# A fused attention and MLP layer on one core: a new lead-in, projections over pairs of blocks, and a new order of instructions

## The chip, the cores and the metric

The kernel runs on one NeuronCore of a Trainium2 chip. The metric is the device time of one execution in microseconds, the median of several. A profile shows the span from the first to the last instruction of one execution; the device time is some 2.6 us longer (215.04 against a span of 212.4 here).

Names of the engines: PE is TensorE (matrix products; PEld its weight loads), DVE is VectorE, ACT is ScalarE, POOL is GpSimd, SP is SyncE, which here only issues DMAs.

## The reference: what is computed

```python
S, D, F, H, W, dil = 2048, 640, 1536, 32, 8, 2      # bf16 inputs
xn  = layernorm(x)                                  # (x - mean) / sqrt(var + 1e-5), no scale or shift
qkv = xn @ wqkv                                     # [2048, 1920], 32 heads of 20
# each position attends to itself and to 7 earlier ones, 2 apart (masked where before the start)
logits[h, s, w] = q[h, s] . k[h, s - 2*w] * 20**-0.5
o[h, s] = sum_w softmax_w(logits)[h, s, w] * v[h, s - 2*w]
out = x + o @ wo + gelu_tanh(xn @ w1 + b1) @ w2 + b2
```

The two branches, attention and MLP, share the normalised input and are added to the residual x.

## The kernel before

The 2048 rows are cut into four chunks of 512 rows, and each chunk into four blocks of 128. Work on TensorE is in bf16 with the contraction over five slices of 128 columns (KT = 5). After normalisation, a block has to be transposed so that the 640 columns lie on the partitions: in chunk 0 by TensorE (`tp`) and a copy out of PSUM (`tc`), in chunks 1 to 3 by a transposing DMA (`td`).

The loads at the start, in the order of issue:

```python
    nc.sync.dma_start(x_sb[:, 0, :], x_nb[:, 0, :])          # block 0
    nc.scalar.dma_start(x_sb[:, 1, :], x_nb[:, 1, :])        # block 1, another queue
    for s in range(3):                                       # q, k, v: 800 KB each
        nc.sync.dma_start(wqkv[s][:], wqkv_v[:, :, s * D : (s + 1) * D])
        if s == 1:
            nc.sync.dma_start(x_sb[:, 2:BPC, :], x_nb[:, 2:BPC, :])
    nc.sync.dma_start(b1_rt[0:FT, :], ...)
    for cs in (slice(BPC, 2 * BPC), slice(2 * BPC, NCH * BPC)):   # blocks 4-7, 8-15
        nc.sync.dma_start(x_sb[:, cs, :], x_nb[:, cs, :])
    nc.sync.dma_start_transpose(b1_t[:], b1_rt[:])
    nc.sync.dma_start(w1_sb[:], ...)                         # all of w1, 1920 KB
    # ... w2, wo and b2 are loaded later, after chunk 1's transposes
```

The normalisation and the transposes of chunk 0, a block at a time (`bn_stats`/`bn_aggr` on VectorE, root on ScalarE, reciprocal and normalisation on VectorE):

```python
    def do_tp(n, bl, a, b):
        xn = tiles["xn", n, bl]
        tp = get(("tp", n, bl), lambda: psA.tile([P, 2 * CH], BF16, tag="acc", name="tp"))   # one tile a block
        for t in range(a, b):
            nc.tensor.transpose(tp[:, t * P : (t + 1) * P], xn[:, t * P : (t + 1) * P], ident[:])

    def do_tc(n, bl, a, b):
        ...
        nc.scalar.copy(xnT[:, a:b, bl * P : (bl + 1) * P], tiles["tp", n, bl][:, a * P : b * P]...)
```

The projections of chunk 0 go a block at a time, each matmul with 128 moving columns; five groups of output tiles per block:

```python
GROUPS = (((0, 0, 4),), ((1, 0, 4),), ((0, 4, 5), (1, 4, 5)), ((2, 0, 4),), ((2, 4, 5),))   # (q/k/v, from, to)

    def do_gj(bl, g, a, b):
        cs = slice(bl * P, (bl + 1) * P)
        ps = get(("gps", bl, g), lambda: psA.tile([P, BPC, P], F32, tag="acc", name="gps"))
        ...
            nc.tensor.matmul(ps[:, i, :], lhsT=wqkv_p[which][:, ti, to, :],
                             rhs=tiles["xnT", 0][:, ti, cs], start=..., stop=...)
```

In chunks 1 to 3 a projection (`pj`) and in all chunks the first MLP layer (`f1`) are groups of five matmuls with 512 moving columns. The output of a block (`o`) is 17 matmuls of 512 (`lo`) and 17 of 128 (`hi`): 12 for the MLP's second layer and 5 for wo. VectorE multiplies q by shifted k (`qk`), TensorE sums the heads (`lg`, tile `L`), VectorE and ScalarE make the softmax, the attention is expanded over the partitions by a DMA (`xd`, `xs`), VectorE multiplies it with shifted v (`av`) and adds (`ad`, `ot`).

Before everything 44 matmuls on zeros (`idle`) keep TensorE busy until the first data arrive; the zeros are written by VectorE:

```python
    zeros = consts.tile([P, P], BF16, name="zeros")
    nc.vector.memset(zeros[:], 0.0)
    ...
        for _ in range(WARM):                                # 44
            nc.tensor.matmul(idle[:, 0, :], lhsT=zeros[:], rhs=zeros[:], start=True, stop=True)
```

The residual goes to the output by DMA: x is stored (`xp`), the bias b2 is added to it in DRAM by an accumulating DMA (`xb`), and each block's result is added in the same way (`od`). The last block instead adds on VectorE and is stored.

The order of all these pieces on every engine is not written by hand. A planner in the kernel (`Plan`) holds each piece with an estimated duration, a rank, what it needs and which buffers it holds; it walks through time, starts on each engine the piece of lowest rank that can start, and the kernel's instructions are emitted in that order. Each engine then runs its instructions in exactly this order and waits where something isn't ready.

```python
RANK = {"av1": 36.4, "av2": 74, "f12": 4.1, ..., "xn0": -14.7}     # 21 offsets, by kind of piece and chunk
    for name, n in (
        ("acc", 4), ("L", 1), ("O", 1), ("xnT", 3), ("q", 2), ("k", 2), ("v", 2), ("prod", 4),
        ("e", 1), ("attn", 1), ("ax", 1), ("oT", 1), ("hT", 18), ("osb", 2), ("xn", 2), ...
```

`acc` are the four PSUM banks that projections, first layer and transposes share; `L` and `O` are for logits and outputs.

Of the kernel before, what the change touches and what calls it, by code (L numbers as in the profile page):

```python
# [15 lines left out]
PE, VE, SE, DQ = "pe", "ve", "se", "dq"  # L16


class Plan:
# [8 lines left out]
    LAG = {PE: 0.22, VE: 0.08, SE: 0.1, DQ: 0.0}  # L28
# [4 lines left out]

    def pool(self, name, n):
        self.pools[name] = n

    def add(self, name, engine, us, rank, needs, fn, bufs=(), after=0.0, table=None, slack=0.0):
        t = {
            "name": name,
            "eng": engine,  # L40
            "us": us,
            "rank": rank + self.offsets.get(name[: 4 if name[:2] in ("pj", "pc", "ad") else 3], 0.0),
            "needs": list(needs),
            "fn": fn,
            "bufs": list(bufs),
            "after": after,
            "table": table,
            "slack": slack,
            "i": len(self.tasks),
        }  # L50
        self.tasks.append(t)
        self.by[name] = t
        for b in bufs:
            self.bufs.setdefault(b, set()).add(name)
        return name

    def run(self):
        end, left, held = {}, list(self.tasks), {p: {} for p in self.pools}
        remaining = {b: set(u) for b, u in self.bufs.items()}
        free = {PE: 0.0, VE: 0.0, SE: 0.0, DQ: 0.0}  # L60
        now, started, table = 0.0, [], "sqrt"
        running, slacks = [], {t["slack"] for t in self.tasks}
        while left:
            done = [t for t in running if t["end"] <= now + 1e-9]
# [7 lines left out]
            while moved:  # L72
                moved = False
                for eng in (PE, VE, SE, DQ):
# [34 lines left out]
            nxt = [f for f in free.values() if f > now + 1e-9]  # L109
            for late in slacks:  # L110
# [20 lines left out]
EPS = 1e-5  # L131
MASKED = -1e9
# [4 lines left out]
GROUPS = (((0, 0, 4),), ((1, 0, 4),), ((0, 4, 5), (1, 4, 5)), ((2, 0, 4),), ((2, 4, 5),))  # L137
# [4 lines left out]
    "av1": 36.4, "av2": 74, "f12": 4.1, "f13": 69.4, "gj1": 19.4, "gj2": -19.4, "o02": -8.9, "o10": 15.3,  # L142
    "o12": -3.3, "o13": -11.3, "o20": 117, "o31": 57.5, "o33": 85.2, "ot0": 20, "pj22": -106.4, "pj31": -13.1,
    "qk1": -4.8, "qk2": 4.4, "st2": 164.2, "st3": 219.3, "xn0": -14.7,
# [3 lines left out]
def make_plan(fns, offsets=RANK):  # L148
# [10 lines left out]

    def done(n, which):  # L160
        if n:
            return [f"pc{n}{which}{to}" for to in range(KT)]
        return [f"gc{bl}{g}" for bl in range(BPC) for g, parts in enumerate(GROUPS) if which in [p[0] for p in parts]]

    pl.add("b1", VE, 0.1, -90, [], f("b1"), after=21.0)
    for n in range(NCH):
# [6 lines left out]
        for bl in range(BPC):  # L173
            land = (4.0, 4.0, 9.6, 9.6)[bl] if n == 0 else (0.0, 13.3, 17.1, 17.1)[n]
            r = -40 if n else -99
            pl.add(f"st{n}{bl}a", VE, 0.5, r, [], f("st", n, bl, 0), after=land)
            pl.add(f"st{n}{bl}", VE, 0.62, r, [f"st{n}{bl}a"] + ([f"rc{n}{bl - 1}"] if n == 0 and bl else []), f("st", n, bl, 1))
            if n == 0:
                pl.add(f"rs{n}{bl}", SE, 0.35, -99, [f"st{n}{bl}"], f("sqrt", n, bl, bl + 1), table="sqrt")
                pl.add(f"rc{n}{bl}", VE, 0.17, -99, [f"rs{n}{bl}"], f("rstd", n, bl, bl + 1))  # L180
# [3 lines left out]
        for bl in range(BPC):  # L184
            xn, tp = ("xn", n, bl), ("acc", "tp", n, bl)
            if n > 0:
                pl.add(f"xn{n}{bl}", SE, 0.81, early + -4.0, [f"rc{n}"], f("xn", n, bl), [xn])
                pl.add(f"tc{n}{bl}", DQ, 4.0 if n > 1 else 2.7, early - 3.0, [f"xn{n}{bl}"], f("td", n, bl), [xn, xnT], 21.5)
                continue

            for i, (a, b) in enumerate(((0, 2), (2, KT)) if bl == 0 else ((0, KT),)):
                u = "a" if b < KT else ""
                us = (b - a) / KT
                pl.add(f"xn{n}{bl}{u}", VE, 0.06 + 0.36 * us, -99, [f"rc{n}{bl}"], f("xn", n, bl, a, b), [xn])
                pl.add(f"tp{n}{bl}{u}", PE, (0.54 if bl == 0 else 0.3) * us, -99, [f"xn{n}{bl}{u}"], f("tp", n, bl, a, b), [xn, tp])
                pl.add(f"tc{n}{bl}{u}", SE, 0.16 + 0.49 * us, -99, [f"tp{n}{bl}{u}"], f("tc", n, bl, a, b), [tp, xnT])
        if n == 1:
            pl.add("ld", DQ, 9.2, -1000, [f"tc1{bl}" for bl in range(BPC)], f("ld"))
        pl.add(f"xp{n}", DQ, 0.3, base + 30, ["ld"], f("xp", n))
        pl.add(f"xb{n}", DQ, 0.0, base + 33, [f"xp{n}"], f("xb", n))  # L200

        if n == 0:
            for bl in range(BPC):
                for g, parts in enumerate(GROUPS):
                    ps, last = ("acc", "g", bl, g), max(p[0] for p in parts)
                    tos = sum(p[2] - p[1] for p in parts)
                    land = (6.4, 8.7, 11.8)[last]
                    r = -50 + (last == 2)
                    need, cut = [f"tc0{bl}"], 0
                    if bl == 0 and g == 0:  # L210
                        cut = 2
                        need.append(pl.add("ga00", PE, 0.112 * tos, r, ["tc00a"], f("gj", bl, g, 0, cut), [xnT, ps], land))
                    pl.add(f"gj{bl}{g}", PE, 0.056 * (KT - cut) * tos, r, need, f("gj", bl, g, cut, KT), [xnT, ps], land)
                    pl.add(f"gc{bl}{g}", SE, (0.27, 0.54, 0, 0.54)[tos - 1], -50, [f"gj{bl}{g}"], f("gc", bl, g), [ps] + [(q, k, v)[p[0]] for p in parts])
# [543 lines left out]
```

## Time and profile before

| | |
|---|---|
| device time, median of 3 runs | 215.04 us (214.53 to 215.87) |
| span of the profiled execution | 212.4 us |
| TensorE busy | 206.9 us (97%) |
| VectorE busy | 174.4 us (82%) |
| ScalarE busy | 109.5 us (52%) |
| DMA traffic | 23.95 MB, mean 113 GB/s |
| granted TensorE clock | 1.000 |

The profile is a page with: the busy time of each engine; the span in 40 slices, each digit the busy share of a slice in tenths; the chain of work that ended last, followed back from the last instruction to what released it; and groups of instructions by line of the kernel, with what ended the idle time before them. The trace behind it can be asked for a timeline: start and length in us, engine, line, operation, output<-inputs, number of instructions, and in square brackets the idle time before them and what ended it. A line such as L501 is a line of the kernel; L501 is the matmul of `do_gj`, L484 of `do_pj`, L653 of `do_f1`, L684 and L686 of `do_o`, L557 of the logits, L437 the transposes, L725 the matmuls on zeros.

### The profile page before, as it was taken

To read this page: it belongs to the slowest core of one execution; us is meant where nothing else is said; L and a number is where in the kernel's file an instruction comes from. 1 tells how busy PE (TensorE), PEld (TensorE's weight loads), DVE (VectorE), ACT (ScalarE), POOL (GpSimd) and SP (SyncE) were. 2 spreads that over 40 slices of the span, in tenths; PEclk is the share of its full clock that TensorE was granted. 3 is DMA by queue.
4 is the path that set the end of the run, shared out by engine and by line. 5 is a ranking of instruction groups with operands and counts; after the bars stand their busy time and mean duration, and the time that the engine had idled before them with its cause. 6 is when DMAs were issued, how large, how long until landed. Compare 5 with 4: busy or idle time off the path is not lost.

```text
span 212.4 us, 3961 instructions
## 1 busy us (share of the span) xinstructions
PE 206.9 (97%) x1670; PEld 121.7 (57%) x1693; DVE 174.4 (82%) x178; ACT 109.5 (52%) x193; POOL 19.7 (9%) x37
## 2 busy tenths in 40 slices
PE   8999999999999999999999999999999999999994
PEld 8799845655545555555555555455555455555552
DVE  3579999759999997599996999999999999972001
ACT  3568997798574654931353883503752511341120
POOL 2000000000020024101100010101110011101130
PEclk9999999999999999999999999999999999999999
DMA  6999528916829199993120027202114611122214
GB/s 216 365 362 376 93 50 275 322 24 132 206 64 163 37 287 196 197 195 89 15 30 0 0 31 200 31 3 31 14 21 48 180 19 22 27 29 31 34 16 76
DMA packets 23465, 23.95 MB, mean 113 GB/s; under 512 B 9112, under 2 KB 20632, under 8 KB 23448
## 3 DMA queue, kind: packets, MB, share of 16 engines
q1 hardware_dynamic: 17864, 16.49, 28.3%
q0 software_dynamic: 4144, 4.92, 17.2%
q10 hardware_dynamic: 1440, 2.29, 3.9%
q8 instruction: 13, 0.21, 0.4%
q14 instruction: 4, 0.03, 0.1%
HBM read 10.00 MB, written 7.54 MB: 83 GB/s over the span
## 4 chain that ended last, share of the span: by engine, by line
PE 97%; issue 1%; DVE 0%; ACT 0%
PE lo L684 27%; PE hps L653 24%; PE pps L484 23%; PE gps L501 8%; PE hi L686 8%; PE L L557 4%; PE idle L725 2%; PE tp L437 1%; ACT xnT L441 0%; DVE osb L714 0%; DVE zeros L361 0%
## 5 line engine op out<-in xcount | busy, mean ns | idle before, releaser
L653 PE MATMUL hps<-xnT,w_sb 128*128 128x512 bf16 x235 | 54.1, 379 | 0.3
L684 PE MATMUL lo<-w_sb,hT 128*128 128x512 bf16 x183 | 51.8, 379 | 0.0
L631 DVE TENSOR_TENSOR pv<-vT,ax 128x2560 bf16<-128x2560 bf16 x32 | 45.9, 1484 | 1.7 <-PE L L557 1.7
L535 DVE TENSOR_TENSOR prod<-qT,kT 128x2560 bf16<-128x2560 bf16 x32 | 45.4, 1484 | 0.0
L686 PE MATMUL hi<-w_sb,hT 128*128 128x128 bf16 x192 | 40.3, 219 | 0.6 <-issue 0.2
L664 ACT ACTIVATE hT<-hps,b1T 128x512 bf16<-128x512 f32 x48 | 31.6, 687 | 17.0 <-PE hps L653 13.3
L653 PEld LDWEIGHTS <-w_sb 128*128 128x128 bf16 x240 | 23.0, 98 | 26.7
L640 DVE TENSOR_TENSOR pv<-pv 128x5120 bf16<-128x5120 bf16 x12 | 33.9, 2825 | 0.4
L684 PEld LDWEIGHTS <-hT 128*128 128x128 bf16 x192 | 18.7, 98 | 22.8 <-issue 0.6
L691 ACT CAST osb<-lo 128x512 bf16<-128x512 f32 x15 | 8.8, 585 | 44.0 <-issue 28.0
L697 POOL DMA_DIRECT2D out_dram<-osb x15 | 12.9, 863 | 110.5 <-ACT osb L692 110.5
L684 PE MATMUL lo<-wo,oT 128*128 128x512 bf16 x79 | 23.0, 379 | 0.0
L686 PEld LDWEIGHTS <-hT 128*128 128x128 bf16 x192 | 18.4, 98 | 1.5
L398 DVE BATCH_NORM_STATS2 stats<-x_sb 128x6 f32<-128x320 bf16 x32 | 14.0, 469 | 5.1 <-DMA x_sb<-in_A_x_dram 5.1
L484 PE MATMUL pps<-xnT,wq_sb 128*128 128x512 bf16 x71 | 16.9, 380 | 0.2
L484 PE MATMUL pps<-xnT,wv_sb 128*128 128x512 bf16 x73 | 16.9, 379 | 0.1
L686 PE MATMUL hi<-wo,oT 128*128 128x128 bf16 x80 | 16.9, 219 | 0.1
L484 PE MATMUL pps<-xnT,wk_sb 128*128 128x512 bf16 x73 | 16.8, 379 | 0.1
L705 DVE TENSOR_TENSOR osb<-lo,x_sb 128x512 bf16<-128x512 f32 x1 | 0.7, 692 | 16.1 <-PE lo L684 16.1
L520 ACT CAST qT<-pps 128x512 bf16<-128x512 f32 x15 | 8.8, 585 | 9.2 <-PE pps L484 9.2
L684 PEld LDWEIGHTS <-oT 128*128 128x128 bf16 x80 | 7.8, 98 | 9.4
L484 PEld LDWEIGHTS <-wk_sb 128*128 128x128 bf16 x75 | 8.7, 118 | 7.3 <-issue 0.2
(62 smaller groups left out, 205.9 us busy)
## 6 DMA issues: line engine op xcount, KB each, us to landing
w_sb<-in_B_w_dram SPq DMA_DIRECT2D x2, 1920.0 KB, 9.2
out_dram<-osb POOLq DMA_DIRECT2D x15, 160.0 KB, 3.4
ax<-attn SPq DMA_DIRECT2D x8, 256.0 KB, 5.4
ax<-attn ACTq DMA_DIRECT2D x8, 256.0 KB, 5.6
out_dram<-x_sb SPq DMA_DIRECT2D x3, 640.0 KB, 4.3
out_dram<-b2bc POOLq DMA_DIRECT2D x3, 640.0 KB, 8.2
x_sb<-in_A_x_dram SPq DMA_DIRECT2D x1, 1280.0 KB, 13.3
wq_sb<-in_A_wqkv_dram SPq DMA_DIRECT2D x1, 800.0 KB, 4.8
```

The lines of the kernel that those rows point to most:

```text
L398: nc.vector.bn_stats(stats[:, i, :], x_sb[:, b, i * (D // 2) : (i + 1) * (D // 2)])
L484: nc.tensor.matmul(ps[:], lhsT=wqkv_p[which][:, ti, to, :], rhs=xnT[:, ti, :], start=(ti == 0), stop=(ti == KT - 1),)
L501: nc.tensor.matmul(ps[:, i, :], lhsT=wqkv_p[which][:, ti, to, :], rhs=tiles["xnT", 0][:, ti, cs], start=(ti == 0 and (i == 0 or b == KT an ...
L520: nc.scalar.copy(dest[:, to, off : off + CH], tiles["pps", n, which, to][:])
L535: nc.vector.tensor_tensor(out=prod[:, i, :, :], in0=qkv_tile(n, 0)[:], in1=qkv_tile(n, 1)[:, :, off : off + CH], op=ALU.mult,)
L631: nc.vector.tensor_tensor(out=pv[:, i, :, :].rearrange("p t (j c) -> p t j c", j=BPC), in0=qkv_tile(n, 2)[:, :, off : off + CH].rearrange( ...
L640: nc.vector.tensor_tensor(out=ta[:], in0=ta[:], in1=tb[:], op=ALU.add)
L653: nc.tensor.matmul(ps[:], lhsT=w1_sb[:, ti, ft * P : (ft + 1) * P], rhs=tiles["xnT", n][:, ti, :], start=(ti == 0), stop=(ti == KT - 1),)
L664: nc.scalar.activation(hT[:], tiles["hps", n, ft][:], ACT.Gelu_apprx_tanh, bias=b1T[:, ft : ft + 1], scale=1.0)
L684: nc.tensor.matmul(lo[:], lhsT=lhs, rhs=rhs[:, 0:CH], start=first, stop=last)
L686: nc.tensor.matmul(hi[:, 0 : D - CH], lhsT=lhs, rhs=rhs[:, CH:D], start=first, stop=last)
L697: nc.gpsimd.dma_start(rows, tiles["osb", n, bl][:], accum_op=ALU.add)
```

## The change: what it does and what it is for

The change has four parts.

- **A new lead-in.** Blocks 0 and 1 are loaded one after the other on SyncE's queue, followed by q's weights in five loads, one for each slice of the contraction, then blocks 2 and 3, k's weights in two loads, v's. The statistics of block 1 go to ScalarE (a sum and a sum of squares by accumulating activations), so that they run beside those of block 0 on VectorE. The two parts of block 0's transposes get PSUM tiles of their own (those of the outputs, free at that time), and VectorE copies one part while ScalarE copies the other. The matmuls before the first data use a constant that GpSimd writes anyway. The purpose is an earlier first projection.
- **Pairs of blocks.** Except q of blocks 0 and 1, the projections of chunk 0 run over pairs of blocks, with 256 moving columns: fewer and longer matmuls.
- **w1 in two halves** ahead of rows 1024 to 2047 of x, so that the first layer of chunk 0 can start earlier.
- **A new order.** The planner now models how long the residual's DMAs take (`xp`, `xb`) and puts them behind the transposes of all chunks; GpSimd's additions get a queue of their own in the plan; the outputs no longer wait for the residual in the plan; and the ranks are set for single pieces (65 offsets), so that the order on every engine is a different one.

The core of the diff (the planner's bookkeeping and repeated parts are cut):

```diff
-GROUPS = (((0, 0, 4),), ((1, 0, 4),), ((0, 4, 5), (1, 4, 5)), ((2, 0, 4),), ((2, 4, 5),))
+COLS = ((0, 2), (2, 4), (4, 5))
@@ RANK @@
-    "av1": 36.4, "av2": 74, "f12": 4.1, "f13": 69.4, "gj1": 19.4, ...
+    "ad01": 563.3, "av010": 52.9, "av1": -25.6, "f10": 111.2, "f100": 9.9, "f101": -71.1, ...
@@ the plan: chunk 0's statistics, normalisation and transposes @@
+            if n == 0 and bl == 1:
+                pl.add("sm", SE, 0.72, -99, [], f("sum1"), after=land)
+                pl.add("nm", SE, 0.22, -99, ["sm"], f("neg1"))
+                pl.add("me", VE, 0.12, -98, ["sm"], f("mean1"))
+                pl.add("sq", SE, 0.93, -99, ["nm"], f("sq1"))
+                pl.add("rs01", SE, 0.3, -99, ["sq"], f("sqrt", 0, 1, 2), table="sqrt")
+                pl.add("rc01", VE, 0.16, -99, ["rs01", "me"], f("rstd", 0, 1, 2))
+                continue
...
+                for u, a, b, eng, own in (("a", 0, 2, VE, "lo"), ("b", 2, KT, SE, "hi")):
+                    us = (b - a) / KT
+                    pl.add(f"xn00{u}", VE, 0.06 + 0.5 * us, -99, ["rc00"], f("xn", 0, 0, a, b), [xn])
+                    pl.add(f"tp00{u}", PE, 0.54 * us, -99, [f"xn00{u}"], f("tp", 0, 0, a, b, own), [xn])
+                    pl.add(f"tc00{u}", eng, 0.16 + 0.49 * us, -99, [f"tp00{u}"], f("tc", 0, 0, a, b, eng), [xnT])
...
+            for u, a, b, eng in (("a", 0, 2, VE), ("b", 2, KT, SE)) if bl == 1 else (("", 0, KT, SE),):
+                pl.add(f"tc0{bl}{u}", eng, 0.16 + 0.49 * (b - a) / KT, -100 if bl == 1 else -99, [f"tp0{bl}"], f("tc", 0, bl, a, b, eng), [tp, xnT])
@@ the plan: residual and outputs @@
-        pl.add(f"xp{n}", DQ, 0.3, base + 30, ["ld"], f("xp", n))
-        pl.add(f"xb{n}", DQ, 0.0, base + 33, [f"xp{n}"], f("xb", n))
+        pl.add(f"xp{n}", DQ, 4.3, base + 30, ["ld"], f("xp", n))
+        pl.add(f"xb{n}", DQ, 8.2, base + 33, [f"xp{n}"], f("xb", n))
...
-                need = [last] if last else [f"ge{n}{ft}" for ft in range(FT)] + [f"xb{n}", "ld"]
+                need = [last] if last else [f"ge{n}{ft}" for ft in range(FT)] + ["ld"]
...
-            pl.add(f"od{n}{bl}", SE, 0.0, base, [f"oc{n}{bl}"], f("od", n, bl), [ob])
+            pl.add(f"od{n}{bl}", GQ, 0.9, base, [f"oc{n}{bl}", f"xb{n}"], f("od", n, bl), [ob], hold=2.6)
@@ the plan: chunk 0's projections @@
+            pl.add("ga", PE, 0.056 * 10, -60, ["tc00a"], f("ga", 0, 2), [xnT, A, B], wq)
+            pl.add("gb2", PE, 0.056 * 5, -60, ["tc00b", "ga"], f("ga", 2, 3), [xnT, A, B], wq)
...
+            pl.add("gd", PE, 0.056 * 10, -59, ["tc01a", "gb4"], f("gd", 0, 2), [xnT, B, C], wq)
+            pl.add("ge", PE, 0.056 * 15, -59, ["tc01b", "gd"], f("gd", 2, KT), [xnT, B, C], wq)
...
+            for which, buf, land in ((0, q, wq), (1, k, wk), (2, v, wv)):
+                for pair in range(0 if which else 1, 2):
+                    for g, (a, b) in enumerate(COLS):
+                        ps = ("acc", "gp", which, pair, g)
+                        nm = pl.add(f"hj{which}{pair}{g}", PE, 0.55 * (b - a), -50 + which // 2, turned(0, pair), f("gp", which, pair, a, b), [xnT, ps], land)
+                        pl.add(f"hc{which}{pair}{g}", SE, 0.3 * (b - a), -50, [nm], f("gq", which, pair, a, b), [ps, buf])
...
-            pl.add(f"f1{n}{ft}", PE, 1.08, base + 10.0 + 1.0 * ft, [...], f("f1", n, ft), [xnT, ps], 22.5)
+            pl.add(f"f1{n}{ft}", PE, 1.08, base + 10.0 + 1.0 * ft, turned(n), f("f1", n, ft), [xnT, ps], 15.8 if ft < FT // 2 else 18.5)
@@ the loads @@
-    nc.sync.dma_start(x_sb[:, 0, :], x_nb[:, 0, :])
-    nc.scalar.dma_start(x_sb[:, 1, :], x_nb[:, 1, :])
-    ...
+    load_x(0, 1)
+    load_x(1, 2)
+    for t in range(KT):
+        load_w(0, t, t + 1)
+    load_x(2, 3)
+    load_x(3, BPC)
+    load_w(1, 0, 2)
+    load_w(1, 2, KT)
+    load_w(2)
     nc.sync.dma_start(b1_rt[0:FT, :], B_b1.rearrange("(t p) -> t p", p=P))
-    for cs in (slice(BPC, 2 * BPC), slice(2 * BPC, NCH * BPC)):
-        nc.sync.dma_start(x_sb[:, cs, :], x_nb[:, cs, :])
+    load_x(BPC, 2 * BPC)
+    for c in range(2):
+        cs = slice(c * F // 2, (c + 1) * F // 2)
+        nc.sync.dma_start(w1_sb[:, :, cs], w1_v[:, :, cs])
     nc.sync.dma_start_transpose(b1_t[:], b1_rt[:])
-    nc.sync.dma_start(w1_sb[:], B_w1.rearrange("(t p) n -> p t n", p=P))
+    load_x(2 * BPC, NCH * BPC)
@@ block 1's statistics on ScalarE @@
+    def do_sum1():
+        nc.scalar.activation(trash()[:], x_sb[:, 1, :], ACT.Identity, accum_out=acc1[:])
+    def do_neg1():
+        nc.scalar.activation(neg1[:], acc1[:], ACT.Identity, scale=-RD / D)
+    def do_sq1():
+        nc.scalar.activation(trash()[:], x_sb[:, 1, :], ACT.Square, bias=neg1[:], scale=RD, accum_out=mv[:, 1, 1:2])
@@ transposes and copies @@
-        tp = get(("tp", n, bl), lambda: psA.tile([P, 2 * CH], BF16, tag="acc", name="tp"))
+        pool, tag = (psO, own) if own else (psA, "acc")
+        tp = pool.tile([P, 2 * CH], BF16, tag=tag, name="tp")
...
+        copy = nc.vector.tensor_copy if eng == VE else nc.scalar.copy
@@ projections over pairs @@
+    def do_gp(which, pair, a, b):
+        ps = psA.tile([P, 2, 2 * P], F32, tag="acc", name="gps")
+        tiles["pair", which, pair, a] = ps
+        for to in range(a, b):
+            for ti in range(KT):
+                nc.tensor.matmul(
+                    ps[:, to - a, :],
+                    lhsT=wqkv_p[which][:, ti, to, :],
+                    rhs=tiles["xnT", 0][:, ti, pair * 2 * P : (pair + 1) * 2 * P],
+                    start=(ti == 0),
+                    stop=(ti == KT - 1),
+                )
@@ the matmuls before the first data @@
+        ones = nc.const_aps.tensor(1.0, [P, P], BF16)
...
-            nc.tensor.matmul(idle[:, 0, :], lhsT=zeros[:], rhs=zeros[:], start=True, stop=True)
+            nc.tensor.matmul(idle[:, 0, :], lhsT=ones, rhs=ones, start=True, stop=True)
```

## The prediction

> **What bounds the kernel now.** I read the page first: the share of each engine and the slices of the span.
>
> ```profile
> PE 206.9 (97%) x1670; PEld 121.7 (57%) x1693; DVE 174.4 (82%) x178; ACT 109.5 (52%) x193; POOL 19.7 (9%) x37
> PE   8999999999999999999999999999999999999994
> PEclk9999999999999999999999999999999999999999
> GB/s 216 365 362 376 93 50 275 322 24 132 206 64 163 37 287 196 197 195 89 15 30 0 0 31 200 31 3 31 14 21 48 180 19 22 27 29 31 34 16 76
> PE 97%; issue 1%; DVE 0%; ACT 0%
> ```
>
> TensorE is busy from the second slice to the last, and the chain that ended last (the fifth line) lies on it for 97%. A busy TensorE can hide slow issue, so I then took the same chain in order of time and divided.
>
> ```profile
> 0.99 4.87 PE idle L725 x44
> 5.87 0.72 PE tp L437 x5
> 6.61 0.38 ACT xnT L441
> 7.03 1.28 PE gps L501 x20
> 8.31 0.43 PE tp L437 x5
> 8.74 4.00 PE gps L501 x70
> ...
> 16.37 8.65 PE gps L501 x155
> 25.03 0.22 PE hps L653
> ...
> 46.88 3.45 PE hps L653 x16
> ...
> 208.69 0.96 PE hi L686 x17
> ```
>
> 8.65 us / 155 is 56 ns for a matmul 128 columns wide, 3.45 / 16 is 216 ns for one of 512. From 25.03 to 209.65 (208.69 + 0.96) stand 240 + 225 + 272 = 737 wide matmuls (first layer, projections, low output halves), 272 narrow ones and 320 of the logits, whose stretches in the chain add to about 9.5 us: 737 x 0.216 + 272 x 0.056 + 9.5 = 183.9 us, of 184.6. So after 25 us the kernel has at most 0.7 us of stalls. Only the lead-in can give: 300 projection matmuls x 0.056 = 16.8, and 15 transposes x 0.056 = 0.8, are 17.6 of the 18.0 us from 7.03 to 25.03. What remains is the start itself. The timeline shows what sets it:
>
> ```profile
> 0.74 0.40 SPq L341 DMA_DIRECT2D x_sb<-in_A_x_dram  x1
> 3.71 0.89 DVE L398 BATCH_NORM_STATS2 stats<-x_sb 128x6 f32<-128x320 bf16 x2 [2.77 <-DMA x_sb<-in_A_x_dram]
> 4.87 0.30 ACT L404 ACTIVATE std<-mv,eps_t 128x1 f32<-128x1 f32 x1 [2.18 <-DVE mv L400]
> 5.40 0.63 DVE L424 TENSOR_SCALAR xn<-x_sb,mv,rstd 128x256 bf16<-128x256 bf16 x2
> 5.80 0.77 PE L437 MATMUL tp<-ident,xn 128*128 128x128 bf16 x5
> 6.61 0.75 ACT L441 COPY xnT<-tp 128x256 bf16<-128x256 bf16 x2 [1.44 <-PE tp L437]
> 7.03 1.28 PE L501 MATMUL gps<-xnT,wq_sb 128*128 128x128 bf16 x20 [0.46 <-ACT xnT L441]
> ```
>
> Block 0 lands, is normalised, transposed and copied; the first copy starts at 6.61, though its two transposes should have ended near 6.1: it waits for all five, which share a PSUM tile.
>
> **What the Trainium skill says.** "TensorE: Matmul & The Clock Gate", Back-to-back issue gap, gives N/2.4 + 2.5 ns for a warm matmul of N columns; 56 and 216 ns here agree, so I take its 109 ns for N = 256, which no matmul of the kernel before shows alone. The same section's lower streaming figure for N = 512 (131 ns) is contradicted by the 216. Part 1 of that page has cold matmuls at 107 ns: 44 dummies in 4.87 us agree. "DMA: Bandwidth & Descriptors", Issuing engines are not separate DMA queues, says that transfers issued by several engines share the same 16 DMA engines; here the first two block loads, from two queues, landed 2.9 and 3.1 us after issue, about together, which fits. "ScalarE: Activation LUTs", What ACT_TABLE_LOAD costs, has back-to-back ACTIVATEs overlap by about 93 ns; the normalisation of 640 columns is 924 ns long and starts again after 820, which agrees.
>
> **The change, part by part.**
>
> Loads. In the first 4 us 160 GB/s moved, 640 kB, which at 365 GB/s is 1.75 us: the stream began near 2.25. Blocks 0 and 1 are 328 kB, done at 3.15, and the statistics began at 3.71: some 0.5 us from last byte to user. With these three numbers, by cumulated bytes on one queue: block 0 usable at 2.25 + 0.45 + 0.5 = 3.2 (0.5 earlier), block 1 at 3.65, q's weights at 5.9 (before: issued at 1.20 + 4.8 = 6.0), k's at 9.0, v's at 11.3, rows 4-7 at 13.1, the halves of w1 at 15.8 and 18.5 (before, 13.27 + 9.2 = 22.5), rows 8-15 at 22.0 (before about 18.3). Five weight loads cost four more issues of about 0.46 us; the last leaves SyncE near 3.5, in time for 5.9.
>
> Block 0. From the start of the statistics to the end of their aggregation (4.63 + 0.21 = 4.84 in the timeline) it took 1.13: now 3.2 to 4.33. The root must wait on ScalarE for block 1's sum (640 columns, 0.92): 3.65 + 0.92 = 4.6, root 0.30, to 4.9. From the root's end to the first normalised part took 0.575 (5.17 to 5.745): 5.48. Two transposes about 0.35, a copy of 256 columns (0.37 on ScalarE before; I assume the same on VectorE), handovers 0.15: first projection at 6.35 instead of 7.03. **Gain 0.7.** The dummies now read a constant and start perhaps 0.2 earlier; they would end near 5.5 and don't decide.
>
> Second copy. ScalarE runs sum, root, negated mean, square, root, copy: 4.9 + 0.25 + 0.92 + 0.3 + 0.48 = 6.9. The first ten q matmuls end at 6.35 + 0.56 = 6.9. No stall, no margin.
>
> Block 1. Normalised 0.75 after its root (6.4): 7.15; transposed by 7.5, under q's matmuls (to 8.1). VectorE has two statistics (0.44 each) ahead of its copy: 7.95 to 8.35. Block 1's q starts at 8.4: stall 0.3, against about 0.35 before, at block 1's transposes (0.43 for five that need 0.28, and a late first group). **Even.** q of blocks 0 and 1 ends at 8.4 + 25 x 0.056 = 9.8.
>
> Pairs. k's first ten, 256 wide, take 10 x 0.109, to 10.9. Blocks 2 and 3: statistics left 2 x 0.65 to 9.65, then reciprocal, the head sums (0.27), two normalisations 0.45, to about 11.1: stall 0.3. Work: 50 x 0.056 + 125 x 0.109 = 16.4 instead of 16.8. **Gain 0.4**, less the stall 0.3.
>
> Sum: from 11.2 remain 16.4 - 2.8 - 1.1 = 12.5 of projections and 0.6 of transposes, so the projections would end at 24.3, had they all been run first, against 25.03: 0.7 us. The after kernel mixes first-layer groups among them, which w1's earlier halves allow; that is the same TensorE work in another order.
>
> Middle. The order of instructions moves a lot, the counts don't: 240, 225, 272, 272, 320 again, and 11 ScalarE table loads again. There is at most 0.7 us of stalls to remove and I expect about 0.3 less or more. The residual copies and bias adds, before between chunk 2's and chunk 3's transposes, now follow all transposes: in the chain before no DMA appears, so this is worth 0 by itself. The tail (0.29 us of VectorE, a store, 2.4 us to the last landing) is unchanged; block 14's add starts some 3.4 us before the last matmul's end and needs 0.2 + 0.86 + 3.4, which still ends before the last store's landing.
>
> Total: -0.7 to -1.0 us.
>
> **Rivals.** (1) VectorE becomes the bound at chunk 1's logits. Rows 8-15 land 3.7 us later, their four blocks of statistics take 4.2, so products start at 26.3 instead of 23.0, and two more products now precede the first logits of chunk 1. Sum: 26.3 + 8 x 1.40 + 4.5 (chunk 3's statistics) + 2.7 (mask, maximum, subtraction) + 2.6 (exp with table load) + 3.8 (sums, reciprocal, attention) + 6 x 1.40 = 59.5. TensorE's work ahead of these logits is 16.4 of projections, 0.8 of transposes, 12 + 15 + 5 = 32 groups of five wide matmuls x 1.08 = 34.6, and 2.35 of logits; from 6.35 with 0.6 of stalls that is 61.1. Margin 1.6; if loads are 3 us later than summed, the time is 216.5.
> (2) ScalarE can't empty PSUM fast enough between 17 and 36 us. 12 gelu x 0.59, eight copies, four normalisations and three table loads x 1.3, with root and pads, are about 18.3 us against 19.5 of TensorE work. Tight, but 24 to 30 us before had ScalarE at 5.97 of 6.00 without a stall on TensorE. If it fails: +0.5 to +1.
> (3) The ScalarE chain of block 1 is late, since it has no margin: each 0.1 us shows on TensorE, at worst eating the 0.7: 215.0.
> (4) The time is hidden anyway, because the middle waits for VectorE at fixed places: against it, TensorE's 0.7 us of stalls.
>
> **Range and chances.** 215.04 - 0.85 is 214.2. The kernel before itself spread over 1.3 us in three runs, and rivals 2 and 3 add up to 1: 213.2 to 215.4 should hold it. 2% is 4.3 us. No step can gain that; losing it needs a wait I haven't seen, in the new queue order.
>
> **What would show it.** Right: the first q matmul near 6.35, block 0's first copy without waiting for five transposes, the matmuls over pairs at 109 ns, stalls of about 0.3 before block 1's q and before blocks 2 and 3's transposes, the last matmul near 208.8. Wrong: stalls of TensorE on VectorE before the logits of chunk 1, on ScalarE between 20 and 36 us, block 0's statistics still at 3.7, or pairs slower than two singles.

## The result, and the profile after

The changed kernel takes 217.31 us (median, 216.78 to 217.72), the kernel before 215.09 (214.53 to 215.87): a ratio of 1.0098, with a 95% interval of 1.0069 to 1.0127. It is 2.2 us slower. The prediction was 214.2, between 213.2 and 215.4: a gain of 0.7 to 1.0 us. The kernel lost more than twice that instead.

The page of the changed kernel: busy time of each engine, then the slices, then the shares of the chain that ended last.

```profile
PE 206.4 (96%) x1543; PEld 121.4 (56%) x1568; DVE 173.9 (81%) x177; ACT 111.3 (52%) x191; POOL 19.7 (9%) x37
PE   8779999999999999999999999999999999999994
GB/s 169 275 365 363 208 32 0 234 365 45 99 160 18 46 30 59 300 259 195 177 31 23 17 242 83 80 30 34 27 8 44 181 8 29 27 32 0 34 61 61
PE 65%; DVE 16%; ACT 7%; DMA 4%; SPq 3%; issue 2%; ACTq 1%; DVEq 0%
```

TensorE has two weak slices, the second and the third (5.4 to 16 us), where before only the first was weak. In the second slice the transfers lag: 275 GB/s, where before it had 365. The chain now leaves TensorE for a third of its length. That is not a third of the time lost: at a wait of only 0.2 us at 86.40 the chain steps to ScalarE, and from there it runs back over ScalarE and VectorE to 48 us, while TensorE was busy most of that time; the same happens at the wait at 33.62 shown below.

The timeline of the changed kernel: start, length, engine, line, operation, and in brackets the idle time before and what ended it.

```profile
1.67 2.32 SPq L387 DMA_DIRECT2D wq_sb<-in_A_wqkv_dram  x5
3.15 0.89 DVE L451 BATCH_NORM_STATS2 stats<-x_sb 128x6 f32<-128x320 bf16 x2 [3.15 <-DMA x_sb<-in_A_x_dram]
5.64 0.29 DVE L512 COPY xnT<-tp 128x256 bf16<-128x256 bf16 x1
5.98 1.00 PE L564 MATMUL gps<-xnT,wq_sb 128*128 128x128 bf16 x15
7.09 0.76 PE L564 MATMUL gps<-xnT,wq_sb 128*128 128x128 bf16 x10
7.96 0.49 DVE L451 BATCH_NORM_STATS2 stats<-x_sb 128x6 f32<-128x320 bf16 x1 [1.23 <-DMA x_sb<-in_A_x_dram]
8.66 0.49 DVE L451 BATCH_NORM_STATS2 stats<-x_sb 128x6 f32<-128x320 bf16 x1 [0.21 <-DMA x_sb<-in_A_x_dram]
9.07 0.27 DVE L512 COPY xnT<-tp 128x256 bf16<-128x256 bf16 x1
9.40 1.56 PE L564 MATMUL gps<-xnT,wq_sb 128*128 128x128 bf16 x25 [1.55 <-DVE xnT L512]
11.33 0.41 PE L595 MATMUL gps<-xnT,wk_sb 128*128 128x256 bf16 x2 [0.38 <-DMA wk_sb<-in_A_wqkv_dram]
12.69 1.07 PE L595 MATMUL gps<-xnT,wk_sb 128*128 128x256 bf16 x8 [0.94 <-DMA wk_sb<-in_A_wqkv_dram]
```

The start came as intended: statistics at 3.15, first copy at 5.64 without waiting for five transposes, first projection at 5.98 instead of 7.03. Then the statistics of blocks 2 and 3 wait for their loads until 7.96 and 8.66, block 1's copy stands behind them on VectorE, and block 1's q starts only at 9.40: 9.40 - 7.09 - 10 x 0.056 = 1.75 us of stall. Then k's weights are late, twice: 11.33 - 9.40 - 25 x 0.056 = 0.53, and 12.69 - 11.33 - 2 x 0.109 = 1.14. Their second part landed at 12.64; the whole of them landed at 8.59 in the kernel before.

Later there are two short waits. One is for a PSUM bank, which ScalarE empties late:

```profile
28.84 4.48 PE L743 MATMUL hps<-xnT,w_sb 128*128 128x512 bf16 x19
33.62 1.24 PE L743 MATMUL hps<-xnT,w_sb 128*128 128x512 bf16 x5 [0.30 <-ACT hT L754]
```

One matmul's record is missing (the groups are of five), so the gap is 33.62 - 28.84 - 20 x 0.216 = 0.46; another 0.2 lies ahead of a later projection, at 86.40.

Account of the last matmul's end: gained 1.05 (first projection) and 0.4 (pairs), lost 1.75 + 1.67 + 0.46 + 0.2 = 4.1, less the 0.35 that the kernel before lost at block 1's transposes; net +2.3. Measured, from the chains in order of time, of the kernel before (shown in the prediction) 208.69 + 0.96 = 209.65 and of the kernel after:

```profile
211.16 0.96 PE hi L776 x17
```

This ends at 212.12: +2.47. Between the medians of the device time it is 2.2, since each trace is one execution. (The 2.6 us that the part ahead of the prediction gives between span and device time set the median against the span of one execution. Within one execution it is about 2 us in both kernels: 214.49 with a span of 212.4 before, 217.0 with 215.0 after.)

Why are the loads late? Busy time of the engines in stretches of 2 us; the last three columns are the granted clock, the DMA share and GB/s. First the kernel before, then after:

```profile
4.00:6.00 2.00, 2.00 (x20) 1.72 (x17) 1.93 (x8) 0.30 (x1) 0.00 (x0) 1.00 1.06 375
6.00:8.00 2.00, 1.54 (x23) 1.31 (x22) 1.02 (x5) 0.95 (x3) 0.00 (x0) 1.00 1.05 372
```

```profile
4.00:6.00 2.00, 1.96 (x22) 1.68 (x20) 1.49 (x7) 1.93 (x8) 0.00 (x0) 1.00 0.92 252
6.00:8.00 2.00, 1.85 (x30) 1.75 (x30) 0.65 (x3) 1.10 (x4) 0.00 (x0) 1.00 0.86 258
12.00:14.00 2.00, 1.31 (x16) 1.30 (x17) 0.00 (x0) 0.20 (x1) 0.00 (x0) 1.00 1.09 383
```

While the short loads are in the queue, 252 to 258 GB/s move instead of 372 to 375, though the DMA engines look busy (0.92, 0.86). Once only long loads are left the rate is 383. From 8 to 10 and from 10 to 12 us, with k's two loads, it is 301 and 314. SyncE's issues start every 0.47 us ((3.56 - 1.67) / 4 in the chain of this trace), which would feed 164 kB / 0.47 us = 347 GB/s; so the pace of issue alone does not give 255. "DMA: Bandwidth & Descriptors", Bandwidth, of the Trainium skill has the rule to batch DMAs to 1 MiB and more for 75% of the peak. It comes from single loads issued by GpSimd, and these are loads issued by SyncE, 800 KB before and 160 KB now; the trace agrees in direction, with 372 to 375 GB/s and 252 to 258.

### The profile page after: what moved, and what is told of

Its sections match the earlier page's. It is cut to its first block, busy times and chain, and to the rows that moved or that the text cites. A ratio compares the mean times of both kernels' runs of the same rounds, so it can differ in the third digit from the quotient of the medians.

```text
span 215.0 us, 3707 instructions
## 1 busy us (share of the span) xinstructions
PE 206.4 (96%) x1543; PEld 121.4 (56%) x1568; DVE 173.9 (81%) x177; ACT 111.3 (52%) x191; POOL 19.7 (9%) x37
## 4 chain that ended last, share of the span: by engine, by line
PE 65%; DVE 16%; ACT 7%; DMA 4%; SPq 3%; issue 2%; ACTq 1%; DVEq 0%
PE lo L774 25%; PE hps L743 17%; PE pps L551 11%; PE hi L776 8%; DVE pv L721 5%; DMA x_sb<-in_A_x_dram 4%; DVE prod L625 4%; PE L L647 3%; SPq L387 2%; DVE stats L451 1%; ACT hT L754 1%; ACT L754 1%; DVE attn L695 1%; ACTq L705 1%; PE gps L595 1%
## 5 line engine op out<-in xcount | busy, mean ns | idle before, releaser
L743 PE MATMUL hps<-xnT,w_sb 128*128 128x512 bf16 x233 | 55.0, 379 | 0.7 <-ACT hT L754 0.3
L451 DVE BATCH_NORM_STATS2 stats<-x_sb 128x6 f32<-128x320 bf16 x30 | 12.9, 468 | 12.8 <-DMA x_sb<-in_A_x_dram 12.8
L774 PE MATMUL lo<-wo,oT 128*128 128x512 bf16 x74 | 21.7, 379 | 0.1
L532 POOL DMA_DIRECT2D out_dram<-b2bc x4 | 5.3, 1322 | 100.7 <-DMA out_dram<-x_sb 100.5
L610 ACT CAST vT<-pps 128x512 bf16<-128x512 f32 x15 | 8.7, 586 | 9.5 <-PE pps L551 7.9
L551 PEld LDWEIGHTS <-wq_sb 128*128 128x128 bf16 x75 | 8.8, 117 | 7.4
```

The lines of the kernel that those rows point to most:

```text
L451: nc.vector.bn_stats(stats[:, i, :], x_sb[:, b, i * (D // 2) : (i + 1) * (D // 2)])
L551: nc.tensor.matmul(ps[:], lhsT=wqkv_p[which][:, ti, to, :], rhs=xnT[:, ti, :], start=(ti == 0), stop=(ti == KT - 1),)
L610: nc.scalar.copy(dest[:, to, off : off + CH], tiles["pps", n, which, to][:])
L743: nc.tensor.matmul(ps[:], lhsT=w1_sb[:, ti, ft * P : (ft + 1) * P], rhs=tiles["xnT", n][:, ti, :], start=(ti == 0), stop=(ti == KT - 1),)
L774: nc.tensor.matmul(lo[:], lhsT=lhs, rhs=rhs[:, 0:CH], start=first, stop=last)
```

## The experiments

Two theories stood at the start: the loads (A: the short loads on one queue slow the stream, and everything behind is late) and the order on VectorE (B: block 1's copy stands behind statistics whose data is late). C in the expectations is that the pairs or the later order lose the time; D, E and F came up on the way and are explained where they are used. Times are medians, with the ratio to the kernel before on the same chip and its 95% interval. In some executions of several kernels, the kernel before among them, the mean granted clock is 0.992 instead of 0.998 to 1.000 and the time 1 to 2 us longer; where they move a median, the times at full clock stand beside it. The first two experiments are the changed kernel with one part undone.

**q's weights in one load.**

```diff
-    for t in range(KT):
-        load_w(0, t, t + 1)
+    load_w(0)
```

> The changed kernel with q's weights in one load instead of five; everything else, the order of instructions too, stays. Theory A (short loads: each of the loads of 160 KB in series on one queue loses some 0.2 us, so that blocks 2 and 3 and k's weights arrive 1.3 to 3 us later than the bytes alone need): the rate between 3 and 11 us rises from about 265 GB/s to over 330, block 2 is usable near 6.9 instead of 7.96, k's second load near 10 instead of 12.69, the wait of block 1's q (1.7 us) falls below 0.6 and the waits for k's weights (0.6 and 1.2) below 0.5 together; 214.3 to 215.0 us against 217.3. Theory B (the order on VectorE alone is to blame): the waits for k's weights stay, 216 to 217. Theory C (pairs, or the new order after the lead-in): no change, 217.3.

216.92 us, 1.0066 [1.0033, 1.0098]: only 0.4 below the changed kernel, where A had 214.3 to 215.0. (The one run at full clock took 215.86.) q's weights landed at 7.97, 2 us later than in the kernel before. The timeline, then stretches of 2 us:

```profile
8.02 1.79 PE L563 MATMUL gps<-xnT,wq_sb 128*128 128x128 bf16 x15 [2.06 <-DMA wq_sb<-in_A_wqkv_dram]
```

```profile
6.00:8.00 2.00, 0.00 (x0) 0.00 (x0) 0.61 (x2) 0.48 (x2) 0.00 (x0) 0.89 1.01 347
8.00:10.00 2.00, 1.98 (x19) 1.99 (x20) 0.94 (x2) 0.00 (x0) 0.00 (x0) 0.50 1.06 371
10.00:12.00 2.00, 2.00 (x28) 1.92 (x26) 1.07 (x4) 1.20 (x3) 0.00 (x0) 0.76 1.07 365
```

The rate is back at 347 to 371, and no wait for k is left, so A holds in that and B, which had these waits stay, does not, though the time is the one it gave. But the first projection waits 2.06 us and then runs at half clock (0.50, then 0.76). So what the weights of k gained was lost at those of q, by a second fault in the order of the queue that this run alone could not name.

**Block 1's copy ahead of the statistics on VectorE** (the five loads kept).

```diff
-    tp01  st02a  st03a  ...  tc01a
+    tp01  ...  tc01a  st02a  st03a        # VectorE's order; st = statistics, tc = copy
```

> The changed kernel with block 1's copy on VectorE moved ahead of the first statistics of blocks 2 and 3, which wait for their loads; the loads stay as they are. Theory B: block 1's q starts near 7.7 instead of 9.4 and the whole kernel gains that 1.7 us, 215.6. Theory A: block 1's q starts early as well, but then TensorE waits longer for k's weights, whose second load still lands at 12.6; the wait only moves, the second part of k's first group starts at 12.7 as before, and the time stays at 217.3 within 0.4.

217.44 us, 1.0091 [1.0056, 1.0126].

```profile
8.13 1.55 PE L564 MATMUL gps<-xnT,wq_sb 128*128 128x128 bf16 x25 [0.27 <-DVE xnT L512]
9.80 0.41 PE L595 MATMUL gps<-xnT,wk_sb 128*128 128x256 bf16 x2
12.25 1.07 PE L595 MATMUL gps<-xnT,wk_sb 128*128 128x256 bf16 x8 [2.04 <-DMA wk_sb<-in_A_wqkv_dram]
```

Block 1's q starts at 8.13 instead of 9.40, and the 1.3 us so gained are spent waiting for k (12.25 instead of 12.69). B as a cause of the lost time falls: its wait covered one that was behind it.

**Both**, 

> Both: q's weights in one load, and block 1's copy ahead of the statistics. Theory A: as the run with one load, and the rest of the wait of block 1's q (0.3 to 0.6 us) goes if k's weights are there by then: 214.0 to 214.8. Theory B: 215.6, no better than the reordering alone.

216.49 us, 1.0051 [1.0016, 1.0086], where A had 214.0 to 214.8; in its trace q's weights land at 8.43, and the first projection starts at 8.47, after a wait of 1.72. Mending both is not enough.

**The kernel before, with q in five loads and nothing else.**

```diff
-    q: nc.sync.dma_start(wqkv[0][:], wqkv_v[:, :, 0:D])
+    for t in range(KT):
+        nc.sync.dma_start(wqkv[0][:, t:t+1, :], wqkv_v[:, t:t+1, 0:D])
```

> The kernel before with only one thing of the change: q's weights in five short loads on SyncE's queue, the other loads and all instructions as they were. Theory A: k's weights land 1 to 2 us later than 8.59 and v's later than 11.75, rate between 3 and 8 us below 320 GB/s, TensorE waits for k's weights of block 0 at about 8.7: 216 to 217 against 215.1. Theories B and C: the loads don't matter by themselves, 215.1 within 0.4.

217.94 us, 1.0121 [1.0081, 1.016]. The three runs at full clock took 216.94, 216.95 and 217.41: 1.9 us above the kernel before, so this part alone costs about as much as the whole change (2.2). k's first matmuls in the kernel before, and here:

```profile
8.64 1.31 PE L501 MATMUL gps<-xnT,wk_sb 128*128 128x128 bf16 x20
```

```profile
10.93 1.31 PE L504 MATMUL gps<-xnT,wk_sb 128*128 128x128 bf16 x20 [2.19 <-DMA wk_sb<-in_A_wqkv_dram]
```

**The kernel before, with q in two loads** (slices 0-1 and 2-4), for the size of it.

> The kernel before with q's weights in two loads (two and three slices) instead of one. Theory A with a loss for each load: between one load (215.1) and five (217.9), k's weights land at 9.0 to 9.7 instead of 8.59, 215.3 to 216.2. If the loss comes with the size of a load (under some size each is slow), two loads of 320 and 480 KB stay near 215.1.

216.16 us, 1.0058 [1.0021, 1.0094].

```profile
9.71 1.31 PE L502 MATMUL gps<-xnT,wk_sb 128*128 128x128 bf16 x20 [0.98 <-DMA wk_sb<-in_A_wqkv_dram]
```

One, two and five loads of the same bytes: k's weights land at 8.59, 9.66 and 10.88, TensorE waits for them 0.1 us at most, 0.98 and 2.19, and the time at full clock is 215.05, 216.16 and 216.95. A stands, with a dose and a response. Two loads of 320 and 480 KB lose already, so it does not take loads as short as 160 KB. Nor is it the later issue of k's load alone: that starts 0.5 and 1.94 us later (2.17 and 3.61 against 1.67), but the bytes ahead of it would keep the queue busy until about 5.4 us at 365 GB/s, by the prediction's own sum. The landings are of one execution each; q's single load, behind the same loads on the same queues, landed between 5.93 and 6.56 in six traces.

**The kernel before, with block 1 on SyncE's queue too**, as in the changed kernel, for the second fault.

```diff
-    nc.scalar.dma_start(x_sb[:, 1, :], x_nb[:, 1, :])
+    nc.sync.dma_start(x_sb[:, 1, :], x_nb[:, 1, :])
```

> The kernel before with only block 1's load moved from ScalarE's queue to SyncE's, behind block 0. Theory D: the rate from 3 to 5 us falls below 320 GB/s and q's weights land 1 to 2 us later than 5.99, as in the run with one load for q (7.97); TensorE waits for them and its clock may fall; 216 to 217.5. Theory A: a single queue costs nothing beyond half a microsecond; 215.1 to 215.5.

216.17 us, 1.006 [1.0047, 1.0073]. q's weights land at 7.16 instead of 5.99, and TensorE waits for them 0.90; k's matmuls start at 9.46 instead of 8.64, with a wait of 0.67. The stretch from 3 to 4 us shows where: the kernel before, this run, and the changed kernel with q in one load.

```profile
3.00:4.00 1.00, 1.00 (x12) 1.00 (x11) 0.29 (x1) 0.00 (x0) 0.00 (x0) 1.00 1.03 358
```

```profile
3.00:4.00 1.00, 1.00 (x12) 1.00 (x11) 0.94 (x3) 0.00 (x0) 0.00 (x0) 1.00 0.64 138
```

```profile
3.00:4.00 1.00, 1.00 (x12) 1.00 (x11) 0.89 (x3) 0.32 (x1) 0.00 (x0) 1.00 0.71 119
```

With two short loads in a row on one queue and a long one behind them the stream falls to 119 to 138 GB/s for a microsecond, so 0.6 to 0.7 us of it are lost. With block 1 on ScalarE's queue it stays at 358. Another 0.47 us of q's delay is issue: its load starts at 1.67 instead of 1.20. That a short load costs the stream of its own queue, and another queue fills the hole, fits this but is not shown: in the changed kernel, with q's five short loads behind the same two block loads, the stretch from 3 to 4 us has 230 GB/s, more than with a long load there.

**The changed kernel with block 1 on ScalarE's queue**, q still in five.

```diff
-    load_x(1, 2)
+    nc.scalar.dma_start(x_sb[:, 1:2, :], x_nb[:, 1:2, :])
```

> The changed kernel with block 1 loaded from ScalarE's queue, as before the change; q's weights stay in five short loads on SyncE's. Theory A (short loads lose time by themselves): k's second load still lands after 12 and TensorE still waits for it; 216.8 to 217.5. Theory D (what loses time is that nothing runs beside SyncE's queue while its first loads start; block 1 from a second queue fills that): the rate from 3 to 6 us rises above 330 GB/s, k's second load lands before 11; 215 to 216.

216.51 us, 1.008 [1.0044, 1.0117]; waits of 0.33 before block 1's q and 0.29 for k. At full clock it took 215.59 to 216.73.

**The same and q's slices 1 and 3 on ScalarE's queue as well.**

> The changed kernel with block 1 and the second and fourth of q's short loads on ScalarE's queue, the others on SyncE's. If a short load loses time because its queue runs dry between its last packet and the next load's first, a second queue fills the gap: rate from 3 to 7 us above 320 GB/s, k's second load before 11, 215 to 216. If the loss is in the short loads themselves, whatever the queue: no better than block 1 alone on the second queue, 216.8 to 217.5.

215.84 us, 1.0032 [1.0018, 1.0046]. By the trace, five short loads over two queues cost less than on one: 336 GB/s from 4 to 6 us instead of 259, k's second part landed at 10.35 instead of 10.94, and no wait for k. The times at full clock overlap (215.32 to 216.19 against 215.59 to 216.73). The stretch from 6 to 8 us still has only 276, and w1's second half is awaited for 0.27 at 20.55.

**Block 1 on ScalarE's queue, q in one load, the copy first.**

> The changed kernel with the lead-in's loads as before: block 1 from ScalarE's queue and q's weights in one load, and block 1's copy ahead of the statistics of blocks 2 and 3; pairs, halves of w1 and the new order stay. Theories A and D together (one queue at the start delays q's weights, short loads delay what follows): q's weights land at 6.0 as before instead of 8, TensorE's first q matmul at 6.5 to 7.0, k's second load before 10, no wait for weights over 0.3 us; 213.6 to 214.6, better than before. Theory C (pairs or the new order lose 1 us or more later on): 215.5 or more.

215.03 us, 0.9999 [0.9987, 1.0011]. The loads of the kernel before give its time back, and no more than that (213.6 to 214.6 was expected): q's weights land at 5.93. The first projection is at 6.38; that this is near the prediction's 6.35 is chance, since the statistics start at 3.55 and not at 3.2. What remains:

```profile
8.21 0.29 DVE L511 COPY xnT<-tp 128x256 bf16<-128x256 bf16 x1 [1.08 <-ACT xnT L511]
8.55 1.56 PE L563 MATMUL gps<-xnT,wq_sb 128*128 128x128 bf16 x25 [0.33 <-DVE xnT L511]
11.71 0.51 PE L506 MATMUL tp<-ident,xn 128*128 128x128 bf16 x6 [0.50 <-DVE xn L491]
```

The stall ahead of block 1's q (8.55 - 7.50 - 0.56 = 0.49) comes from the copy on VectorE, which waits for ScalarE's copy of the other part (1.08), and so runs after it instead of beside it. The two copies read one PSUM tile and write one output tile; which of these makes the second wait was not tested. The other stall (0.5 by the row; 11.71 - 9.95 - 10 x 0.109 = 0.67 from the start of the last ten k matmuls) is ahead of the transposes of blocks 2 and 3.

**The order on VectorE repaired**: block 1's copy directly after its transposes and ahead of ScalarE's part, between the statistics of blocks 2 and 3, and the head sums moved to chunk 1; loads as in the last run.

```diff
-        if n == 0 and b1 == BPC:
+        if n == 1:
             constants()
...
+        early = [t for t in order if t["name"] == "tc01a"]
+        order = [t for t in order if t not in early]
+        at = [t["name"] for t in order].index("tp01") + 1
+        order[at:at] = early
```

> The loads of the lead-in as before (block 1 from ScalarE's queue, q's weights in one load), and VectorE's work reordered: block 1's copy after one statistic and ahead of ScalarE's part of the same copy, for which it waited until 8.2 in the run before; the head sums moved from the chain of blocks 2 and 3 to chunk 1's. If what remains of the change (pairs, w1 in halves, new order) is sound and only loads and these two waits ate its gain, the waits of block 1's q (0.5) and of blocks 2 and 3's transposes (0.8) fall below 0.3 together: 213.8 to 214.4, faster than both. Theory C (the new order after the lead-in loses what the pairs gain): 215.0.

215.13 us, 1.0014 [0.9976, 1.0052]. The stalls of the lead-in are gone but for 0.2, and the time did not move: it is that of theory C. The timeline shows where they went:

```profile
20.05 3.41 PE L742 MATMUL hps<-xnT,w_sb 128*128 128x512 bf16 x15 [0.36 <-DMA w_sb<-in_B_w_dram]
27.91 1.28 ACT L471 ACT_TABLE_LOAD   x1
29.52 1.28 ACT L753 ACT_TABLE_LOAD   x1
31.56 1.24 PE L742 MATMUL hps<-xnT,w_sb 128*128 128x512 bf16 x5 [0.52 <-ACT hT L753]
```

TensorE comes earlier to the first layer, and there waits for w1's second half, landed at 20.01, and for a PSUM bank, which ScalarE holds through two table loads around chunk 2's root (F in the expectations).

**The same with q in five loads**, 

> As the run with the repaired order, but q's weights again in five short loads on SyncE's queue. Theory A: k's second load lands near 11 instead of 9.3, TensorE waits 1 to 1.8 us for it, 215.0 to 216.0. If the short loads mattered only through the order of VectorE's work: as with one load, 213.8 to 214.4.

216.8 us, 1.0083 [1.0042, 1.0124], with k's second part awaited for 1.40:

```profile
11.78 1.07 PE L595 MATMUL gps<-xnT,wk_sb 128*128 128x256 bf16 x8 [1.40 <-DMA wk_sb<-in_A_wqkv_dram]
```

Against the run before, the five loads alone are worth 1.7 us by the medians and 1.2 at full clock (216.36 against 215.12).

**The same as the repaired order, with fewer loads** (blocks 2 and 3 in one, k in one), 

> As the run with the repaired order, and also blocks 2 and 3 in one load and k's weights in one. Theory A: the stream gains another 0.2 to 0.4 us, but TensorE no longer waits for it: 213.6 to 214.4, within 0.3 of that run. If it is slower by more, the halves of k's weights were worth their price.

215.51 us, 1.0016 [0.9985, 1.0046]: no further gain, where 213.6 to 214.4 was expected. The loads behind q's were no longer the bound.

**w1's halves swapped** (the repaired order; the half that is used first is loaded first).

```diff
-    for c in range(2):
+    for c in (1, 0):
```

> As the run with the repaired order, but the second half of w1, which the order uses first, is loaded first. Theory E (what the repair gained was lost again at the next load: the first first-layer group waited 0.6 us for w1's second half, landed at 20.0): that wait goes, 214.4 to 214.8. Theory F (from 20 to 36 us ScalarE sets the pace, whatever TensorE does): TensorE waits longer for PSUM banks instead, 215.0 to 215.2.

215.19 us, 0.9999 [0.9979, 1.0019]. The wait for w1 is gone; in its place is one on ScalarE, 0.60 at 22.32, and the one near 32 us is still there, 0.64 at 32.13.

**Chunk 2's root next to chunk 3's** (the repaired order), which spares two of ScalarE's 11 table loads.

```diff
+        for name, after in (("rs2", "ge04"), ("rc2", "st31"), ("xn20", "rc2"), ("tc20", "xn20"), ("xn21", "tc20"), ("tc21", "xn21")):
+            move(name, after)
```

> As the run with the repaired order, but ScalarE takes the root of chunk 2's variance next to that of chunk 3 (its reciprocal and two normalisations move with it), which saves two table loads of 1.28 us between 27 and 31 us. Theory F: the wait of 0.7 us for a PSUM bank near 31 us goes, 214.3 to 214.7. Theory E alone: 215.1.

214.47 us, 0.9997 [0.9959, 1.0035]: unclear by the interval. At full clock (four of six runs) it took 214.14 to 214.52, and the wait near 32 us is gone from its trace.

**Both**, 

> Both. If both waits are real and independent, about 1.2 us less than the repaired order: 213.7 to 214.2, faster than the kernel before. If only one limits at a time: as the better of the two single runs.

**214.32 us** (214.21 to 214.61), the kernel before 215.23; 0.9964 [0.9947, 0.9981]. This is 0.4% less than the kernel before, with an interval clear of 1, and 1.4% less than the changed kernel. The root's move alone took the same at full clock (median 214.36), so that w1's swap adds anything is not shown: both together are as the better of the two. The page and the timeline of this run:

```profile
PE 205.4 (97%) x1543; PEld 120.5 (57%) x1568; DVE 173.9 (82%) x177; ACT 108.6 (51%) x189; POOL 19.7 (9%) x37
PE 86%; DMA 5%; DVE 2%; ACT 2%; SPq 2%; issue 1%
```

```profile
6.53 1.00 PE L563 MATMUL gps<-xnT,wq_sb 128*128 128x128 bf16 x15
7.65 2.12 PE L563 MATMUL gps<-xnT,wq_sb 128*128 128x128 bf16 x35
9.60 1.25 PE L594 MATMUL gps<-xnT,wk_sb 128*128 128x256 bf16 x10
10.89 0.73 PE L506 MATMUL tp<-ident,xn 128*128 128x128 bf16 x10
26.48 5.56 PE L742 MATMUL hps<-xnT,w_sb 128*128 128x512 bf16 x24
```

From 6.53 on TensorE has three stalls of 0.2 to 0.3 us. The table loads are 9 instead of 11 (189 ScalarE instructions for 191).

## Why the prediction was wrong, step by step

**Loads: the step that failed.** It read "by cumulated bytes on one queue at 365 GB/s" and "Five weight loads cost four more issues of about 0.46 us". The issues did cost that (2.32 us for five, last one ended at 3.99, half a microsecond later than said). But the rate was taken from a stream of 800 KB loads and applied to a queue of 160 KB loads, which ran at 252 to 258. The sum gave q's weights at 5.9, k's at 9.0, v's at 11.3 and w1's halves at 15.8 and 18.5. They landed at 7.33, 12.64, 14.86, 19.30 and 22.05: 1.4 us late for q, 3.6 for k. TensorE waited 1.75 us behind the late blocks 2 and 3 and 1.67 for k. The run with q in five in the kernel before shows it alone (+1.9 us at full clock), the one with block 1 on SyncE's queue shows the other part (+1.1). Nothing in the profile before had a queue of short loads in it, so that rate had to be held as unknown. The prediction came near it, with "a wait I haven't seen, in the new queue order" and with loads 3 us late in its first rival, but gave the one no size and saw the other only at chunk 1's logits. (Its check of w1 by the kernel before, 13.27 + 9.2 = 22.5, took the median of two loads; that load landed at 23.16.)

**Block 0: right in mechanism, small error in size.** Statistics at 3.15 (3.2 predicted), first projection at 5.98 (6.35): 0.4 better, about 0.2 of it because block 1's sum, which the root waits for, was done at 4.38 and not at 4.6.

**Second copy, "no stall, no margin".** ScalarE's copy started at 5.98, not 6.4, and did not stall TensorE. Right.

**Block 1, "stall 0.3": wrong by 1.45.** The order (copy behind two statistics) was seen, and the wait was sized with blocks 2 and 3 on hand; their loads were late. With loads back in time (block 1 on the second queue, q in one) and the copy ahead of the statistics the same stall is 0.49, and there it is the two copies that run in turn, which the prediction did not foresee. Its own order with loads in time was not run.

**Pairs, "109 ns": right.** Ten matmuls 256 wide stand every 1.09 us (14.15 to 15.24), so the 0.4 us of work was saved. The stall of "0.3" at blocks 2 and 3 was 0.67 with loads in time, and hidden behind k's in the changed kernel.

**Middle.** "About 0.3 less or more" held in size, 0.66 of stalls. Rival 1 (VectorE at chunk 1's logits) did not occur. Rival 2 (ScalarE between 17 and 36 us) did, in part: 0.46 at 33.62 in the changed kernel. Once the lead-in was mended, a wait of 0.67 on ScalarE (31.56 in that timeline, from the sum of the matmuls before it) and one of 0.52 for w1, a DMA, took back the gain; with w1's halves swapped two waits on ScalarE did. Its "three table loads" were the right place to look. Rival 3 (ScalarE's chain for block 1) did not occur. Rival 4 (the time is hidden anyway) came true in the runs with mended loads, though behind ScalarE and w1 and not behind VectorE: the gain showed only after chunk 2's root was moved.

**The total.** "-0.7 to -1.0" is what the mended version gives (214.32 against 215.23, 214.2 predicted); but it took a second queue, one load for q, another order on VectorE and a moved root that spares two table loads, which is no part of the change. So that the sizes agree is luck: the sum was made for a kernel that is not this one. What the moved root alone would give in the kernel before was not run.

**Not told apart.** The residual DMAs behind the transposes, the pairs and the new order were not run one by one. No DMA of the residual appears in any wait of TensorE in these traces; that it is worth 0 is argued, not shown.

## What to carry to other kernels

A rate measured on long loads does not hold for a queue of short ones: splitting a load so that its first part comes sooner delays all that is queued behind it, and that delay has to be measured and summed too. Two queues recovered a part of it here, and not all (215.84 us, 0.8 above the kernel before). A stall found on an engine may cover another right behind it, so after mending one, look for what the next instruction would have waited for; here mended loads with the copy first took back the 2.2 us, but the time fell below that of the kernel before only when VectorE's order and ScalarE's table loads were mended as well. Whether VectorE's order was needed for that was not run alone.

## What was not expected of the hardware

A second queue matters at the start by more than its issue time. "DMA: Bandwidth & Descriptors", Issuing engines are not separate DMA queues, says that several issuing engines save only the time of issue. Here moving one 160 KB load, with 0.47 us of issue, to the other queue brought the stream in the stretch from 3 to 4 us from 138 to 358 GB/s in the kernel before, and from 100 to 352 in the changed kernel with q in one load and the copy first. The 800 KB load behind it landed 1.2 and 2.5 us earlier, of which 0.47 is issue; the rest contradicts the page. The data packets are of the same size in all these runs (1280 bytes). From 3 to 11 us their median is 55 ns in the kernel before and after, but 5 of 2296 took over 200 ns before, and 55 of 1673 after, some over 1 us. So single packets are slow, not all; why they come with the short loads was not settled.

In the changed kernel with q in one load, a wait of about 2 us for q's weights was followed by half a clock: 0.50 for 3.4 us, from 7.55 to 10.97. "TensorE: Matmul & The Clock Gate", Part 1: The HAM clock gate, puts the drop after at least one idle window of some 3.4 us, with windows that run freely. The length of the drop agrees with it; the gap does not, since at 2.06 us it was shorter than a window (1.72 with the copy first, and the same drop). It was not always so: of that kernel's six runs five had a mean clock of 0.992 and one of 1.000, which was 0.9 to 1.2 us faster. Half a clock for 3.4 of 208 us of TensorE's work is 0.8% of the mean, so 0.992 is about one such drop. The kernel before had 0.992 in 2 of 11 runs (216.05 and 216.62), none of which left a trace; its trace at 1.000 has no such wait, so what brings the drop about there is open.
